# A chunked linear-attention layer with a two-layer SiLU network behind it: r and k turned in two row groups, y turned by DMA, the first chunk written out by hand

## The chip, the cores and the metric

The kernel runs on one core of one Trainium2 chip. The metric is device time in microseconds, from the start to the end of one execution. Three runs of the kernel before gave 225.85, 229.26 and 228.23 us, median 228.23. The profile is of one further execution, with a span of 226.5 us.

The engines are called by their names in the profile: PE is TensorE (matmuls), PEld its weight loads, DVE is VectorE, ACT is ScalarE, POOL is GpSimd, SP is SyncE, which here only issues DMAs. Matmul results land in PSUM[...].

## The reference

Batch 4, 8 heads, 768 tokens, head dimension 48. For each batch and head a state of 48x48 is carried from token to token:

```python
for t in range(S):
    cur = einsum('bhd,bhe->bhde', u[None] * kt, vt)
    y[:, :, t] = einsum('bhd,bhde->bhe', rt, state + cur)
    state = w[None, :, :, None] * state + einsum('bhd,bhe->bhde', kt, vt)
```

Then y is laid out as x, one row of 384 per token (3072 tokens), and goes through a network of two layers without biases:

```python
h = x @ w_in                       # 384 -> 2048
g = h * (1.0 / (1.0 + np.exp(-h))) # SiLU
out = g @ w_out                    # 2048 -> 384
```

## The kernel before, in words

**Chunks and units.** The 768 tokens are cut into six chunks of 128 (C). A unit is one chunk of one batch, all 8 heads; there are 24 (NU), and unit i is chunk i // 4, batch i % 4. Within a chunk the recurrence becomes matmuls: r is scaled by w to the power of the token's place (lamR), k by the inverse (lamK), both after being turned so that the head dimension lies on the partitions. Two heads share one turned block, at partitions 0 to 47 and 64 to 111, so there are four pairs (NP).

**One unit.** `p1_natural` works on untransposed data: v is cast to f16 on ACT, and POOL forms k times u (`ku`, L145), times r (`rku_f`, L147), k decayed to the end of the chunk (`kc`, L148) and, after DVE has summed over the head dimension (`rku`, L151), the bonus term `vu` (L153). `p1` turns r and k on PE, eight transposes of 128x112 against a 128x128 identity (L165), into two PSUM banks; DVE multiplies each with lamR and lamK while it evicts them (L167, L169); from the second chunk on ACT makes an f16 copy of r (L172). `p2` multiplies k and r of each head in f32 (L179 for the head at partition 0, L181 for the one at 64), into two banks, and DVE masks each bank to the strict triangle (`am`, L186). `p3` sums, in PSUM, r times the state (L198, from the second chunk on) and masked product times v (L201), forms the chunk's addition to the state (`sps`, L208), adds `vu` to y on DVE (L211) and updates the state (L215, L221, L224, L225). `p4` turns y on PE, three transposes (L237), and ACT copies the result to xT (L238), where the four batches of one chunk lie side by side.

**The network.** `l1` is one block of 128 hidden units for the four batches of a chunk: three matmuls of 512 columns (L248) and a SiLU on ACT (L251); 16 blocks per chunk. `l2` is four of the 16 matmuls that give one batch's output (L260, 384 columns); the last part copies the sum on DVE (L264) and stores it. So a chunk gives 16 + 16 = 32 pieces of work.

**The order.** Nothing is scheduled: each engine runs its instructions in the order of the program. The loop over units calls the product of unit i, the preparation of unit i + 1, then `p3` and `p4` of unit i, and puts between them, with `fill(n)`, pieces from the list `fillers`. That list gets the 32 pieces of a chunk when the chunk's fourth unit is done, so the pieces of one chunk fill the gaps of the next one, eight per unit; there is none before unit 4, and the pieces of the last chunk run alone at the end:

```python
for i in range(NU):
    p2(i)
    fill(2)
    ...
    load(i + NIN)
    fill(1); p3(i)
    fill(2); p4(i)
    fill(3)
    if b == B - 1:
        fill(len(fillers))
        fillers.extend(moe(sc))
```

**Loads and buffers.** r, k and v of a unit come by SP's queue (192 KB each, L102) into one of four buffers (NIN), unit 0 first, then `w_bc` and `u_bc`, then units 1 to 3; unit i + 4 is asked for once unit i's data is used. The weights come by POOL's queue, which casts them to f16: w_in in three pieces behind the first unit's work (L285), w_out in four during unit 1 (L292). PSUM: three banks for r, k and products (tag tA), two for y, state and turned y, three for the network.

Of the kernel before, what the change touches and what calls it, by code (L numbers as in the profile page):

```python
# [8 lines left out]
FP = mybir.dt.float32  # L9
# [6 lines left out]
def kernel(  # L16
# [11 lines left out]
    nc = tc.nc  # L28
# [12 lines left out]
    NIN = 4  # L41

# [5 lines left out]


    wpT = cst.tile([PR, NP], FP)  # L50
    nc.vector.memset(wpT, 1.0)
    nc.sync.dma_start(out=wpT[0:D, :], in_=bass.AP(tensor=w.tensor, offset=0,
                                                   ap=[[1, D], [PW, NP]]))
    nc.sync.dma_start(out=wpT[64:PR, :], in_=bass.AP(tensor=w.tensor, offset=D,
                                                     ap=[[1, D], [PW, NP]]))
    w_bc = cst.tile([128, HD], FP)
    u_bc = cst.tile([128, H, D], FP)

# [8 lines left out]

    maskM = cst.tile([128, 128], FP)
# [3 lines left out]
        base=-1, channel_multiplier=-1, pattern=[[1, 128]],  # L72
    )
    ident16 = cst.tile([128, 128], F16)
    nc.gpsimd.tensor_copy(out=ident16, in_=ident)


    rin = [big.tile([128, H, 64], FP, name=f"rin{i}") for i in range(NIN)]
    kin = [big.tile([128, H, 64], FP, name=f"kin{i}") for i in range(NIN)]
    vin = [big.tile([128, H, D], FP, name=f"vin{i}") for i in range(NIN)]  # L80
    kc = [big.tile([128, H, 64], F16, name=f"kc{i}") for i in range(2)]
# [5 lines left out]
    st = [big.tile([PR, NP, PW], FP, name=f"st{b}") for b in range(B)]  # L87
    st16 = [big.tile([PR, NP, PW], F16, name=f"stb{b}") for b in range(B)]
    for b in range(B):
        nc.vector.memset(st[b], 0.0)  # L90
    win = [big.tile([128, DFF], F16, name=f"win{q}") for q in range(NQ)]
    wout = big.tile([128, NFT, HD], F16)

    def unit(i):
        return divmod(i, B)

    def load(i):
        if i >= NU:
            return
        sc, b = unit(i)  # L100
        for t, src, wd in ((rin, r, 64), (kin, k, 64), (vin, v, D)):
            nc.sync.dma_start(out=t[i % NIN][:, :, 0:D],  # L102
                              in_=src[b, :, sc * C:sc * C + C, :]
                              .rearrange("h t d -> t h d"))

    load(0)
    nc.sync.dma_start(out=w_bc, in_=bass.AP(tensor=w.tensor, offset=0,
                                            ap=[[0, 128], [1, HD]]))
    nc.sync.dma_start(out=u_bc, in_=bass.AP(tensor=u.tensor, offset=0,
                                            ap=[[0, 128], [D, H], [1, D]]))  # L110
    for i in range(1, NIN):
        load(i)

# [3 lines left out]
    lnw_bc = cst.tile([128, HD], FP)  # L117
    nc.scalar.activation(out=lnw_bc, in_=w_bc, func=AF.Ln)
    eR = cst.tile([PR, NP, C], FP)
    nc.vector.tensor_tensor(out=eR, in0=it_row.unsqueeze(1).broadcast_to([PR, NP, C]),  # L120
                            in1=lnwT.unsqueeze(2).broadcast_to([PR, NP, C]), op=ALU.mult)
# [6 lines left out]
    nc.scalar.activation(out=lamK, in_=eK, func=AF.Exp, scale=-1.0)  # L128
    lamC = cst.tile([128, H, D], FP)
# [5 lines left out]

    live = {}

    def p1_natural(i):

        n = i % NIN  # L140
        L = live.setdefault(i, {})
        L["v16"] = wrk.tile([128, H, D], F16, name="v16", bufs=3)
        nc.scalar.copy(out=L["v16"], in_=vin[n])
        ku = wrk.tile([128, H, D], FP, name="ku")
        nc.gpsimd.tensor_tensor(out=ku, in0=kin[n][:, :, 0:D], in1=u_bc, op=ALU.mult)  # L145
        rku_f = wrk.tile([128, H, D], FP, name="rku_f")
        nc.gpsimd.tensor_tensor(out=rku_f, in0=rin[n][:, :, 0:D], in1=ku, op=ALU.mult)  # L147
        nc.gpsimd.tensor_tensor(out=kc[i % 2][:, :, 0:D], in0=kin[n][:, :, 0:D],  # L148
                                in1=lamC, op=ALU.mult)
        rku = wrk.tile([128, H], FP, name="rku")  # L150
        nc.vector.tensor_reduce(out=rku, in_=rku_f, axis=mybir.AxisListType.X, op=ALU.add)  # L151
        L["vu"] = wrk.tile([128, H, D], FP, name="vu")
        nc.gpsimd.tensor_tensor(out=L["vu"], in0=vin[n],  # L153
                                in1=rku.unsqueeze(2).broadcast_to([128, H, D]),
                                op=ALU.mult)

    def p1(i):
        n = i % NIN
        L = live.setdefault(i, {})
        tr = ps.tile([128, NP, C], FP, tag="tA", bufs=3)  # L160
        tk = ps.tile([128, NP, C], FP, tag="tA", bufs=3)
        for t, src in ((tr, rin), (tk, kin)):
            flat = src[n].rearrange("p h d -> p (h d)")
            for p in range(NP):
                nc.tensor.transpose(t[0:PR, p, :], flat[:, 128 * p:128 * p + PR], ident)  # L165
        L["rT"] = wrk.tile([PR, NP, C], FP, name="rT")
        nc.vector.tensor_tensor(out=L["rT"], in0=tr[0:PR], in1=lamR, op=ALU.mult)  # L167
        L["kT"] = wrk.tile([PR, NP, C], FP, name="kT")
        nc.vector.tensor_tensor(out=L["kT"], in0=tk[0:PR], in1=lamK, op=ALU.mult)  # L169
        if i >= B:  # L170
            L["rT16"] = wrk.tile([PR, NP, C], F16, name="rT16")
            nc.scalar.copy(out=L["rT16"], in_=L["rT"])  # L172

    def p2(i):
        L = live[i]
        ae = ps.tile([128, NP, C], FP, tag="tA", bufs=3)
        ao = ps.tile([128, NP, C], FP, tag="tA", bufs=3)
        for p in range(NP):
            nc.tensor.matmul(ae[:, p, :], L["kT"][0:D, p, :], L["rT"][0:D, p, :],  # L179
                             start=True, stop=True)  # L180
            nc.tensor.matmul(ao[:, p, :], L["kT"][64:PR, p, :], L["rT"][64:PR, p, :],  # L181
                             start=True, stop=True)
        L["am"] = []
        for a in (ae, ao):
            am = wrk.tile([128, NP, C], F16, name="am", bufs=4)
            nc.vector.tensor_tensor(out=am, in0=a,  # L186
                                    in1=maskM.unsqueeze(1).broadcast_to([128, NP, C]),
                                    op=ALU.mult)
            L["am"].append(am)

    def p3(i):
        sc, b = unit(i)
        L = live[i]
        v16 = L["v16"]
        y = ps.tile([128, H, D], FP, tag="y", bufs=2)
        for p in range(NP):
            if sc:
                nc.tensor.matmul(y[:, 2 * p:2 * p + 2, :], L["rT16"][:, p, :],  # L198
                                 st16[b][:, p, :], start=True, stop=False)
            for j in range(2):  # L200
                nc.tensor.matmul(y[:, 2 * p + j, :], L["am"][j][:, p, :],  # L201
                                 v16[:, 2 * p + j, :], start=not sc, stop=(not sc or j == 1))
        if sc < NCH - 1:
            sps = ps.tile([128, NP, PW], FP, tag="y", bufs=2)
            kf = kc[i % 2].rearrange("p h d -> p (h d)")
            vf = v16.rearrange("p h d -> p (h d)")
            for p in range(NP):
                nc.tensor.matmul(sps[0:PR, p, :], kf[:, 128 * p:128 * p + PR],  # L208
                                 vf[:, PW * p:PW * p + PW], start=True, stop=True)
        L["y16"] = wrk.tile([128, H, D], F16, name="y16")  # L210
        nc.vector.tensor_tensor(out=L["y16"], in0=y, in1=L["vu"], op=ALU.add)  # L211
        if sc < NCH - 1:
            if sc:
                sdec = wrk.tile([PR, NP, PW], FP, name="sdec")
                nc.gpsimd.tensor_tensor(out=sdec, in0=st[b],  # L215
                                        in1=wCT.unsqueeze(2).broadcast_to([PR, NP, PW]),
                                        op=ALU.mult)
            for p0, c0 in ((0, 0), (64, D)):
                dst = st[b][p0:p0 + D, :, c0:c0 + D]
                if sc:  # L220
                    nc.vector.tensor_tensor(out=dst, in0=sps[p0:p0 + D, :, c0:c0 + D],  # L221
                                            in1=sdec[p0:p0 + D, :, c0:c0 + D], op=ALU.add)
                else:
                    nc.vector.tensor_copy(out=dst, in_=sps[p0:p0 + D, :, c0:c0 + D])  # L224
            nc.gpsimd.tensor_copy(out=st16[b], in_=st[b])  # L225
# [3 lines left out]
    def p4(i):  # L229
        sc, b = unit(i)  # L230
        L = live.pop(i)
        if sc not in xts:
            xts[sc] = wrk.tile([128, NQ, B, C], F16, name="xT", bufs=2)
        yT = ps.tile([128, NQ, C], F16, tag="y", bufs=2)
        yf = L["y16"].rearrange("p h d -> p (h d)")
        for q in range(NQ):
            nc.tensor.transpose(yT[:, q, :], yf[:, 128 * q:128 * q + 128], ident16)  # L237
        nc.scalar.copy(out=xts[sc][:, :, b, :], in_=yT)  # L238

# [3 lines left out]
    def l1(sc, ft):  # L243
        if ft == 0:
            gts[sc] = wrk.tile([128, NFT, B * C], F16, name="gT", bufs=2)
        hps = ps.tile([128, B * C], FP, tag="moe", bufs=3)
        for q in range(NQ):
            nc.tensor.matmul(hps, win[q][:, ft * 128:(ft + 1) * 128],  # L248
# [91 lines left out]
```

## Time and profile before

| | |
|---|---|
| median of 3 runs | 228.23 us |
| span of the profile | 226.5 us |
| PE busy | 202.3 us (89%) |
| PEld busy | 133.1 us (59%) |
| POOL busy | 119.0 us (53%) |
| DVE busy | 115.8 us (51%) |
| ACT busy | 94.2 us (42%) |
| first matmul of the network | 42.8 us |
| last matmul | 222.8 us |
| DMA, mean over the span | 100 GB/s |

The profile is read in three ways here. The slices cut the span into 40 equal parts and give the busy share of each engine in tenths, PE's granted clock in tenths of full speed, and the share of the DMA engines. The stretches give busy microseconds with the number of instructions in brackets. The chain follows the work that ended last back from the end; each piece has its start, its length and what it was. Matmuls overlap in the pipeline, so the distance between the starts of two of them, not the duration of one, is what a matmul costs.

### The profile page before, as it was taken

The page shows a single profiled execution, that of the slowest core. Times are in us where ns is not written, and L with a number is a line of the kernel's source. Part 1 is how long each engine was busy: PE and PEld are TensorE (multiplying, and loading weights), DVE is VectorE, ACT ScalarE, POOL GpSimd, SP SyncE. Part 2 cuts the span into 40 slices and gives each one's busy share as a digit, 9 for nine tenths or more (in the row PEclk, how much of TensorE's full clock was granted, in tenths as well). Part 3 has the DMA queues.
Part 4 walks back from the last instruction along what each step waited for, and adds up shares of the span by engine and source line. Part 5 has one row for each costly group of instructions (what it writes and reads, how often), then busy time and mean ns, then how long its engine had stood idle before and what let it go on. Part 6 is the DMA issues. An engine that isn't in the chain of part 4 may idle for free.

```text
span 226.5 us, 4378 instructions
## 1 busy us (share of the span) xinstructions
PE 202.3 (89%) x1672; PEld 133.1 (59%) x1672; DVE 115.8 (51%) x225; ACT 94.2 (42%) x173; POOL 119.0 (53%) x150
## 2 busy tenths in 40 slices
PE   1266298799999999999999999999999999999993
PEld 1164177456667656766665776666676557654561
DVE  6157365647368536656833865563685256420020
ACT  2521011586621378411578211866213783029500
POOL 2387975765674665667467466656746561000000
PEclk9999555799999999999999999999999999999999
DMA  5999999992216385026735053923161000110011
GB/s 95 201 196 208 204 185 176 224 186 50 58 38 139 105 177 104 3 76 137 166 77 107 0 142 98 213 48 61 38 142 69 3 0 3 69 53 16 3 69 69
DMA packets 81604, 22.69 MB, mean 100 GB/s; under 512 B 75824, under 2 KB 81200, under 8 KB 81584
## 3 DMA queue, kind: packets, MB, share of 16 engines
q1 hardware_dynamic: 79040, 19.28, 39.3%
q0 software_dynamic: 2544, 3.15, 8.0%
q8 instruction: 13, 0.21, 0.4%
q14 instruction: 7, 0.06, 0.1%
HBM read 20.84 MB, written 4.72 MB: 113 GB/s over the span
## 4 chain that ended last, share of the span: by engine, by line
PE 81%; POOL 8%; DVE 3%; issue 3%; DMA 2%; SPq 1%; DVEq 0%; POOLq 0%
PE hps L248 28%; PE ops L260 28%; PE ae L179 10%; PE tr L165 4%; PE tk L165 4%; PE yT L237 2%; DMA u_bc<-in_u_dram 2%; POOL ku L145 2%; PE y L201 2%; POOL rku_f L147 2%; PE sps L208 2%; PE y L198 2%; POOL wout L292 1%; SPq L102 1%; POOL kc L148 1%
## 5 line engine op out<-in xcount | busy, mean ns | idle before, releaser
L248 PE MATMUL hps<-xT,win 128*128 128x512 f16 x288 | 70.2, 384 | 0.0
L251 ACT ACTIVATE gT<-hps 128x512 f16<-128x512 f32 x96 | 57.4, 598 | 29.5 <-PE hps L248 27.3
L260 PE MATMUL ops<-wout,gT 128*128 128x384 f16 x384 | 69.0, 326 | 0.0
L260 PEld LDWEIGHTS <-gT 128*128 128x128 f16 x384 | 35.8, 98 | 21.2
L248 PEld LDWEIGHTS <-win 128*128 128x128 f16 x288 | 26.7, 99 | 26.5 <-issue 1.3
L186 DVE TENSOR_TENSOR am<-ae,maskM 128x512 f16<-128x512 f32 x24 | 16.6, 691 | 49.1 <-PE ao L181 49.1
L153 POOL TENSOR_TENSOR vu<-vin,rku 128x384 f32<-128x384 f32 x24 | 19.9, 829 | 35.8 <-DVE rku L151 35.8
L179 PE MATMUL ae<-rT,kT 48*128 48x128 f32 x192 | 30.8, 306 | 6.1 <-DVE kT L169 6.1
L179 PEld LDWEIGHTS ae<-rT,kT 48*128 48x128 f32 x192 | 25.8, 206 | 14.2 <-issue 7.5
L264 DVE COPY osb<-ops 128x384 f32<-128x384 f32 x24 | 13.4, 557 | 38.3 <-PE ops L260 37.9
L181 PE MATMUL ao<-rT,kT 48*128 48x128 f32 x192 | 30.8, 306 | 0.0
L238 ACT COPY xT<-yT 128x384 f16<-128x384 f16 x24 | 11.4, 476 | 43.3 <-PE yT L237 43.3
L145 POOL TENSOR_TENSOR ku<-kin,u_bc 128x384 f32<-128x384 f32 x24 | 24.1, 1005 | 7.9 <-DMA u_bc<-in_u_dram 6.7
L172 ACT CAST rT<-rT 112x512 f16<-112x512 f32 x20 | 12.4, 618 | 37.2 <-DVE rT L167 37.2
L181 PEld LDWEIGHTS ao<-rT,kT 48*128 48x128 f32 x192 | 25.8, 206 | 0.0
L147 POOL TENSOR_TENSOR rku_f<-rin,ku 128x384 f32<-128x384 f32 x24 | 24.0, 999 | 1.9
L148 POOL TENSOR_TENSOR kc<-kin,lamC 128x384 f16<-128x384 f32 x24 | 24.0, 999 | 0.8 <-ACT lamC L130 0.8
L225 POOL CAST stb<-st 112x384 f16<-112x384 f32 x20 | 10.1, 503 | 25.0 <-DVE st L221 19.9
L165 PE MATMUL tr<-ident,rin 128*112 128x128 f32 x96 | 16.7, 302 | 5.1 <-DMA rin<-in_r_dram 5.1
L167 DVE TENSOR_TENSOR rT<-tr,lamR 112x512 f32<-112x512 f32 x24 | 16.5, 689 | 4.2 <-PE tr L165 4.2
L151 DVE TENSOR_REDUCE rku<-rku_f 128x8 f32<-128x384 f32 x24 | 13.1, 544 | 10.2 <-POOL rku_f L147 10.1
L165 PEld LDWEIGHTS tr<-ident,rin 128*112 128x112 f32 x96 | 12.5, 147 | 9.0 <-issue 5.9
(46 smaller groups left out, 200.9 us busy)
## 6 DMA issues: line engine op xcount, KB each, us to landing
rin<-in_r_dram SPq DMA_DIRECT2D x24, 192.0 KB, 3.4
kin<-in_k_dram SPq DMA_DIRECT2D x24, 192.0 KB, 3.5
vin<-in_v_dram SPq DMA_DIRECT2D x24, 192.0 KB, 3.6
out_dram<-osb SPq DMA_DIRECT2D x24, 192.0 KB, 1.9
win<-in_moe_w_in_dram POOLq DMA_DIRECT2D x3, 512.0 KB, 8.8
wout<-in_moe_w_out_dram POOLq DMA_DIRECT2D x4, 384.0 KB, 10.3
w_bc<-in_w_dram SPq DMA_DIRECT2D x1, 192.0 KB, 4.3
u_bc<-in_u_dram SPq DMA_DIRECT2D x1, 192.0 KB, 4.1
```

Source lines behind the costliest of these rows:

```text
L145: nc.gpsimd.tensor_tensor(out=ku, in0=kin[n][:, :, 0:D], in1=u_bc, op=ALU.mult)
L147: nc.gpsimd.tensor_tensor(out=rku_f, in0=rin[n][:, :, 0:D], in1=ku, op=ALU.mult)
L148: nc.gpsimd.tensor_tensor(out=kc[i % 2][:, :, 0:D], in0=kin[n][:, :, 0:D], in1=lamC, op=ALU.mult)
L153: nc.gpsimd.tensor_tensor(out=L["vu"], in0=vin[n], in1=rku.unsqueeze(2).broadcast_to([128, H, D]), op=ALU.mult)
L165: nc.tensor.transpose(t[0:PR, p, :], flat[:, 128 * p:128 * p + PR], ident)
L167: nc.vector.tensor_tensor(out=L["rT"], in0=tr[0:PR], in1=lamR, op=ALU.mult)
L179: nc.tensor.matmul(ae[:, p, :], L["kT"][0:D, p, :], L["rT"][0:D, p, :], start=True, stop=True)
L181: nc.tensor.matmul(ao[:, p, :], L["kT"][64:PR, p, :], L["rT"][64:PR, p, :], start=True, stop=True)
L186: nc.vector.tensor_tensor(out=am, in0=a, in1=maskM.unsqueeze(1).broadcast_to([128, NP, C]), op=ALU.mult)
L248: nc.tensor.matmul(hps, win[q][:, ft * 128:(ft + 1) * 128], xts[sc][:, q, :, :].rearrange("p b t -> p (b t)"), start=(q == 0), stop=(q == ...
L251: nc.scalar.activation(out=gts[sc][:, ft, :], in_=hps, func=AF.Silu)
L260: nc.tensor.matmul(ops, gts[sc][:, ft, b * C:(b + 1) * C], wout[:, ft, :], start=(ft == 0), stop=(ft == NFT - 1))
```

## The change

The kernel's order is rewritten, with these parts:

- **r and k turned in two row groups** (`turn`). Each transpose takes 64 tokens instead of 128; the two halves of a pair lie at partitions 0 to 63 and 64 to 127, so they use different rows of PE, and each half writes a bank of its own. The aim is that the halves run side by side. `decay` evicts from this layout.
- **y by DMA from unit 6** (`turn_y`): a transposing DMA on SP's queue writes xT straight from y, in place of three transposes on PE and a copy on ACT. Units 0 to 5 stay on PE.
- **One mask over two banks** (`masked`): the two products lie in one PSUM tile of two banks and are masked by one instruction of 1,024 elements.
- **PSUM** is cut into one pool of two double banks for turned r and k, products, and y with the state's addition (tag att), and four banks for the network.
- **The first chunk by hand**: units 0 to 3 are written out in order. The first layer of chunk 0 runs in half blocks: two hidden blocks of the first two batches in one bank (256 columns each), from unit 2 on; the other half follows as eight pieces in `fillers`. The weights come in four pieces of 512 columns and four of w_out, spread between the units.
- **The start**: one table for ln and exp is loaded at once, w and u come by ACT's queue, the loads of units 0 to 3 are first on SP's; POOL instead of DVE clears the states; DVE instead of POOL decays k in units 0 to 3; the first chunk's state is copied by ACT.
- **Smaller ones**: the state's matmul takes 128 columns of kc instead of 112; the decayed state is formed ahead of its unit; the output's copy moves from DVE to ACT except for the last chunk; the loop gives two and six pieces instead of two, one, two and three, and doesn't empty the list at a chunk's end.

```diff
+    def turn(i):
         n = i % NIN
-        tr = ps.tile([128, NP, C], FP, tag="tA", bufs=3)
-        tk = ps.tile([128, NP, C], FP, tag="tA", bufs=3)
-        for t, src in ((tr, rin), (tk, kin)):
+        t = L(i)["t"] = ps.tile([128, 2, 2, NP, HC], FP, name="t", tag="att", bufs=2)
+        for x, src in enumerate((rin, kin)):
             flat = src[n].rearrange("p h d -> p (h d)")
             for p in range(NP):
-                nc.tensor.transpose(t[0:PR, p, :], flat[:, 128 * p:128 * p + PR], ident)
+                for y in range(2):
+                    rows = slice(HC * y, HC * y + HC)
+                    nc.tensor.transpose(t[0:PR, y, x, p, :], flat[rows, 128 * p:128 * p + PR],
+                                        ident[rows, rows])
...
+    def masked(i):
+        am = L(i)["am"] = wrk.tile([128, 2, NP, C], F16, name="am")
+        nc.vector.tensor_tensor(
+            out=am.rearrange("p h g c -> p (h g) c"), in0=L(i)["a"].rearrange("p h g c -> p (h g) c"),
+            in1=maskM.unsqueeze(1).broadcast_to([128, H, C]), op=ALU.mult)
...
-                nc.tensor.matmul(sps[0:PR, p, :], kf[:, 128 * p:128 * p + PR],
+                nc.tensor.matmul(sps[:, p, :], kf[:, 128 * p:128 * p + 128],
                                  vf[:, PW * p:PW * p + PW], start=True, stop=True)
...
+    def turn_y(i, by_pe):
+        sc, b = unit(i)
+        yf = L(i)["y16"].rearrange("p h d -> p (h d)")
+        x = x_tile(sc)
+        if not by_pe:
+            nc.sync.dma_start_transpose(out=x[:, :, b, :], in_=yf)
+            return
...
+    def l1(sc, b0, nb, ft):
...
+        m = B // nb
+        hps = ps.tile([128, m, nb * C], FP, name="hps", tag="moe", bufs=4)
+        for f in range(m):
+            for q in range(NQ):
+                nc.tensor.matmul(hps[:, f, :], win[:, q, (ft + f) * 128:(ft + f + 1) * 128],
+                                 xts[sc][:, q, b0:b0 + nb, :].rearrange("p b t -> p (b t)"),
+                                 start=(q == 0), stop=(q == NQ - 1))
...
+    bonus_products(0)
+    ld_win(0)
+    turn(0)
+    decay(0)
+    cast_v(0)
+    product(0)
+    turn(1)
+    bonus_sum(0)
+    bonus_v(0)
+    masked(0)
+    decayed_k(0)
+    decay(1)
+    bonus_products(1)
+    ld_win(1)
+    outputs(0)
+    evict_y(0)
+    product(1)
+    turn_y(0, True)
+    state(0)
+    load(4)
...
+    fillers.extend([lambda ft=ft: l1(0, 2, 2, ft) for ft in range(0, NFT, 2)])
+    fillers.extend(second(0))
+
+    for i in range(B, NU):
+        sc, b = unit(i)
+        product(i)
+        if i + 1 < NU:
+            bonus_products(i + 1)
+            decayed_k(i + 1)
+        masked(i)
         fill(2)
         if i + 1 < NU:
-            p1_natural(i + 1)
-            p1(i + 1)
+            turn(i + 1)
+            decay(i + 1)
+        outputs(i)
+        evict_y(i)
+        turn_y(i, i < 6)
+        state(i)
         load(i + NIN)
...
+        fill(6)
         if b == B - 1:
-            fill(len(fillers))
-            fillers.extend(moe(sc))
+            fillers.extend(first(sc) + second(sc))
     fill(len(fillers))
```

## The prediction

> **What bounds the kernel now.** I read the page's forty slices first, then the busy time of three long stretches, the waits of TensorE, and the chain of work, in order of time, through one unit of the steady part.
>
> ```profile
> PE   1266298799999999999999999999999999999993
> PEclk9999555799999999999999999999999999999999
> DMA  5999999992216385026735053923161000110011
> ```
>
> A slice is 5.66 us. TensorE is below full for the first seven or eight and full to the end after that; its clock is at half in slices five to seven; the DMA engines are full in slices two to nine.
>
> ```profile
> 0.00:20.00 20.00, 6.72 (x46) 5.64 (x47) 9.65 (x27) 5.86 (x10) 10.95 (x22) 1.00 0.86 170
> 20.00:42.90 22.90, 15.63 (x137) 12.91 (x137) 12.72 (x26) 4.78 (x9) 16.92 (x21) 0.61 1.14 196
> 42.90:222.80 179.90, 179.90 (x1493) 114.51 (x1492) 92.90 (x172) 83.53 (x155) 91.09 (x108) 0.99 0.36 81
> ```
>
> Columns: stretch, length, busy time of PE, PEld, DVE, ACT and POOL, granted clock, DMA share, GB/s. From 42.9 us TensorE never idles; no other engine is busy much over half of that stretch. Before it TensorE is busy 22 of 43 us, partly at half clock.
>
> ```profile
> PE yT L237 <- DVE y L211: 9.4, 4, 4.5
> PE ae L179 <- DVE kT L169: 6.1, 1, 6.1
> PE tr L165 <- DMA rin<-in_r_dram: 5.1, 1, 5.1
> ```
>
> These are all the waits TensorE has, and all lie in the first 43 us. So there are two accounts: what TensorE has to do, and when it can begin to do it without a break. One steady unit, from the chain:
>
> ```profile
> 59.14 0.30 PE ae L179
> 59.44 0.01 PE ao L181
> 59.45 0.11 PE ae L179
> ...
> 60.23 1.41 PE ops L260 x8
> 61.64 0.44 PE tr L165 x4
> 62.07 0.44 PE tk L165 x4
> 62.51 0.65 PE ops L260 x4
> ...
> 63.54 0.23 PE sps L208 x4
> 63.77 1.30 PE ops L260 x8
> 65.07 0.17 PE yT L237 x3
> 65.23 1.95 PE ops L260 x12
> 67.18 0.30 PE ae L179
> ```
>
> The unit takes 67.18 - 59.14 = 8.04 us: product of k and r 1.09, turning of r and k 0.88, outputs 0.38 (63.16 to 63.54), state 0.23, y turned 0.17, and eight fillers of 0.65 (5.2), of which the one after the product shows 0.11 more.
>
> **What the Trainium skill says.** "TensorE: Matmul & The Clock Gate", Part 1: the clock is halved until the array has been busy for some microseconds, and again after an idle window. The trace agrees: steps of 0.11 us in the product above are 0.21 us at 29 us, with the clock row at 5. The same page, on weight-path perf modes: a fast weight load is taken for 128 weight columns that are not fp32. The trace agrees (weight loads between 60 and 200 us):
>
> ```profile
> L165 PEld LDWEIGHTS tr<-ident,rin 128*112 128x112 f32 x68 | 8.2, 133 | 2.4
> L201 PEld LDWEIGHTS <-am 128*128 128x128 f16 x144 | 7.8, 97 | 1.6
> L208 PEld LDWEIGHTS <-kc 128*112 128x112 f16 x56 | 3.9, 130 | 0.0
> ```
>
> 112 columns take 130 ns in f16 and 133 in f32; 128 columns in f16 take 97. "TensorEngine Tiling (Array Packing)", Key Properties: tiles in different row groups run in parallel, and changing the tiling mode drains the array. Both are in the trace: the even and odd product start 0.01 us apart, and its first step is 0.30 instead of 0.11, with 0.11 more behind the block. Eight pairs at 0.107 would be 0.86; the block costs 1.20. So a block in row groups pays about 0.3 us of entry and exit.
>
> **The change part by part.**
>
> TensorE's account. Warm work before: 179.9 us after 42.9, and before that four whole units of the first chunk plus turn and product of unit 4. A unit of the first chunk is 0.88 + 1.20 + 0.26 (outputs without the state's part, my share of the 0.38) + 0.23 + 0.17 = 2.74; 4 x 2.74 + 0.88 + 1.20 = 13.0. Sum 192.9.
>
> *Turning in two row groups*: 16 transposes of 64 rows by 64 columns in place of 8 of 128, the pair side by side. A transpose of 128 columns takes 0.11 (0.44 for four), so 64 columns 0.055; if the pair is truly parallel, weight loads too, the block is 8 x 0.056 + 0.3 = 0.75. If the two weight loads take turns, each about 0.05 (112 columns in f16 keep a 0.057 pace in the state's four matmuls, 0.23 for four), the pair costs 0.10 and the block 8 x 0.10 + 0.3 = 1.1. Today 0.88 without any switch. I take no change; the bounds are 24 x -0.13 = -3 us and 24 x +0.2 = +5 us.
>
> *y by DMA from unit 6*: 18 x 0.17 = 3.1 us less. *State matmul with 128 weight columns*: the pace falls from 0.057 to 0.04 (96 columns; output matmuls of 96 columns show 0.04 to 0.05), 20 x 0.06 = 1.2 less. *Half blocks*: 256 columns cost half of 512 (0.215), so the sum stays. Work after: 192.9 - 3.1 - 1.2 = 188.6.
>
> Off the path in steady state: one mask over two banks (1,024 elements: 0.69 + 512 / 0.96 = 1.2 us by the scaling of the 512 operations, instead of 0.69 + 0.68) lies under two fillers and the turn, 1.3 + 0.9; the output's copy moved to ScalarE (0.5 us each) finds it with 83.5 of 179.9 us busy, less 0.48 per unit for the xT copy that goes; the shared pool of two double banks asks only for order that the data asks for anyway, since the turn of i+1 reuses what was evicted one filler block earlier. All are hidden by TensorE's 7.5 to 8 us per unit.
>
> The start. Loads are issued first on SyncE, at about 1 us instead of 1.9; w and u go on ScalarE's queue behind one table load (1.28). By the landing of about 2 us for w, 4.1 for u: w at 5, u at 7.5. lnw 5.3, eR 6.1, lamR 6.8 and lamK 7.5 (the second table load, 1.28 at 8.93, is gone, and neither waits for w_bc, which cost 3.5), decay to 8.3: first product at 8.3, against 13.04. The cleared states on GpSimd (eight, about 0.4 each by VectorE's 0.38 today) lie under the wait for u, 6.7 us today. After that the cycle of a first unit is VectorE's: mask 1.2, decayed k 0.55, decay 1.37, then product on TensorE (1.2, up to 2 at half clock) while y and the bonus sum (0.55 each) run: 4.5 to 5.5 us. GpSimd has 1.0 + 1.0 + 0.83 + about 0.8 of issue, less than that; today it carries also kc 1.0, the state's cast and seven issues in lumps of 1.8 and 3.1. Products of units 1 and 2 at about 13.7 and 19; first half blocks at about 21. From there TensorE has per unit 1.2 + 0.88 + 0.5 + 0.17 + 2.6 of half blocks = 5.3, as much as VectorE's cycle, so it is full. With 1.7 us for the clock that rises late: effectively full from 22.7, having done 2 x 2.74 + 0.88 + 1.20 = 7.6.
>
> Bubbles added: the table load before the first Silu, 1 us (1.28, half hidden by four buffers). DMA: until the second layer starts in unit 5, loads 0 to 5 (3.54 MB), w and u (0.4) and both weights (3.15) = 7.1 MB must land; at the 190 to 196 GB/s seen, 37 us, from 2 us on 39; unit 5 is due at about 38. I take 2 us. Unit 7: fillers of chunk 0 are 8 + 16 = 24, used up by units 4 to 6, so unit 7 has none, and chunk 1 can't begin before its y came by DMA. Mask 1.2, outputs 0.4, decay and y 2, transfer 3 to 4, less product 1.2 and turn and next product 2: about 4 us idle. At the other four ends of a chunk six fillers (3.9) and a product (1.2) stand between outputs and the first use of xT: 5.1, against decay's rest and y 1.6 plus the transfer.
>
> *The transfer itself* is in no row. From below: a plain store of 192 KB lands in 1.9 us, so 1.9. From above: "VectorE: DVE Perf Modes", The three transpose paths, prices a 128x128 crossbar transpose at 1309 ns; three one after the other give, as an estimate, 3.9. I take 3.9: 0.4 to 0.7 us of wait, 4 x 0.7 = 2.8. Queued behind it on SyncE are only loads for four units later, which have a unit to spare.
>
> Sum: 22.7 + 188.6 - 7.6 = 203.7; + 1 + 2 + 4 + 2.8 = 213.5 for TensorE's end. The tail (copy and store, 226.5 - 222.8) stays 3.7, giving 217. Counted from the DMA side: second layer at 41, with 26.2 us of work done by then (sixteen half blocks 10.4, five units 13.7, turn and product 2.1): 41 + 188.6 - 26.2 + 4 + 2.8 + 3.7 = 214. The two share their terms; I take 215.
>
> **Rivals.** *The start stays bound by DMA* (0.15): the full DMA row up to slice nine speaks for it; if both weights land as late as today's DMA row ends, 50 us, the end is 50 + 188.6 - 26.2 + 4 + 2.8 + 3.7 = 223. Against it: today nothing of the weights was issued before 13.7, and GpSimd's lumps delayed it. *All parts work* (0.14): parallel transposes (-3), transfer in 1.9 (-2.8, and -2 in unit 7), no DMA bubble (-2): 205. *The transposing transfer becomes the bound* (0.06): two-byte pieces at, say, 9 us each put 5 us on each of five chunk ends and hold the loads behind them; with the turn at its upper bound (+5) and the late DMA that is 223 + 5 x 3 + 5 = 243, slower. Nothing in the profile speaks for it but that no such transfer is in it.
>
> **How the numbers follow.** The forecast has 0.65. Range 205 to 223: it holds the forecast with its bounds (turn -3 to +5), the first two rivals at their ends, and leaves the last out. Two per cent are 223.7 and 232.8: faster 0.88, same 0.07, slower 0.05.
>
> **What would show it.** Right: product of unit 0 at 8 to 9 us, first Silu at 21 to 24, TensorE's slices full from the fifth, one idle gap near unit 7, a unit of 7.5 to 7.9 us. Turn: block time against 0.88. Transfer: time to landing, and waits of the first layer on it once per chunk. Wrong: weights landing after 45 us, first-layer matmuls waiting for xT by more than 2 us at every chunk, or a turn above 1.1 us.

## The result, and the profile after

The changed kernel took 214.36 us (median of 4 runs, 213.84 to 214.56), the kernel before, measured beside it, 228.29. The ratio is 0.942, with a 95% interval of 0.936 to 0.948: faster by about 6%. 215 was predicted. The profiled execution has a span of 212.6 us. Medians here and below are of all runs, while ratios and their intervals leave out executions in a slower state, of which only the kernel before and one experiment on it have some.

The slices of the changed kernel, each 5.3 us long:

```profile
PE   1677898798986999999999999999999999999993
PEclk9999999999998899999999999999999999999999
DMA  6899999999175255277346267525627010220011
```

TensorE is at seven to nine tenths from the third slice, with a dent in the thirteenth (63.8 to 69.1 us), and full after it. The stretches tell how much of each part it was busy (columns as before the change: length, PE, PEld, DVE, ACT, POOL, clock, DMA share, GB/s):

```profile
0.00:22.65 22.65, 12.65 (x127) 10.24 (x127) 14.62 (x29) 6.86 (x16) 17.11 (x33) 1.00 0.94 170
22.65:43.70 21.05, 19.13 (x227) 15.47 (x226) 11.97 (x19) 16.41 (x37) 15.56 (x19) 1.00 1.18 196
43.70:60.60 16.90, 15.65 (x166) 10.23 (x165) 8.29 (x14) 4.38 (x9) 9.25 (x12) 1.00 0.57 122
60.60:69.10 8.50, 5.50 (x72) 3.76 (x74) 5.28 (x8) 2.11 (x4) 6.75 (x9) 0.92 0.77 173
69.10:188.30 119.20, 119.20 (x1163) 72.19 (x1164) 60.62 (x100) 59.22 (x108) 69.40 (x82) 0.99 0.45 100
```

The first matmul of the network starts at 22.65 us instead of 42.8. From there to 69.1 TensorE idles 1.92 + 1.25 + 3.0 = 6.2 us, where before it idled not at all after 42.9; from 69.1 to the last matmul it never idles. Its two longest waits in that part (total, times, longest), and from the chain the work behind the second, at the end of unit 7:

```profile
PE yT L283 <- DVE y L248: 3.2, 3, 1.3
PE hps L295 <- DMA xT<-y: 1.6, 1, 1.6
```

```profile
67.00 2.09 PE hps L295 x6
69.09 1.03 PE t L187 x16
```

A steady unit, from the chain of the changed kernel (start, length, work; the outputs in between are left out):

```profile
98.02 1.09 PE a L207 x16
99.11 1.40 PE hps L295 x6
100.51 0.59 PE t L187 x16
101.10 0.15 PE ys L223
...
101.59 0.17 PE ys L235 x4
101.76 3.88 PE hps L295 x18
105.64 1.09 PE a L207 x16
```

The unit takes 105.64 - 98.02 = 7.62 us, where it was 8.04. The turn of r and k is 0.59 (0.88 before), but in the chain the first output matmul behind it shows 0.15, where the kernel before has this:

```profile
63.16 0.04 PE y L198
```

That is 0.11 more for a block in row groups, and it leaves a net gain of 0.18. The state's four matmuls take 0.17 (0.23), and y's 0.17 is gone. Together these are 0.41, the difference of the units but for rounding. The transfer that took y's place, from the list of DMA issues (count, median us to landing):

```profile
xT<-y SPq DMA_TRANSPOSE x18, 2.3
```

### The profile page after: what moved, and what is told of

Read it like the earlier page. It is cut to its first block, busy times and chain, and to the rows that moved or that the text cites. A ratio compares the mean times of both kernels' runs of the same rounds, so it can differ in the third digit from the quotient of the medians.

```text
span 212.6 us, 4734 instructions
## 1 busy us (share of the span) xinstructions
PE 192.9 (91%) x1858; PEld 122.7 (58%) x1858; DVE 103.0 (48%) x173; ACT 99.0 (47%) x190; POOL 118.1 (56%) x151
## 4 chain that ended last, share of the span: by engine, by line
PE 86%; DVE 5%; DMA 3%; issue 2%; POOL 1%; ACT 0%; ACTq 0%; DVEq 0%; POOLq 0%
PE hps L295 31%; PE ops L307 30%; PE a L207 12%; PE t L187 7%; DMA u_bc<-in_u_dram 2%; PE ys L223 2%; PE ys L228 2%; DVE rT L193 2%; PE ys L235 1%; DMA xT<-y 1%; DVE y L248 1%; PE yT L283 1%; DVE am L212 1%; DVE kT L193 1%; DVE kc L161 1%
## 5 line engine op out<-in xcount | busy, mean ns | idle before, releaser
L295 PE MATMUL hps<-xT,win 128*128 128x512 f16 (+1 forms) x336 | 68.2, 357 | 2.1 <-DMA xT<-y 1.6
L212 DVE TENSOR_TENSOR am<-a,maskM 128x1024 f16<-128x1024 f32 x24 | 29.4, 1224 | 56.1 <-PE a L207 56.0
L207 PE MATMUL a<-rT,kT 48*128 48x128 f32 x384 | 30.6, 304 | 3.4 <-DVE kT L193 3.4
L207 PEld LDWEIGHTS a<-rT,kT 48*128 48x128 f32 x384 | 25.8, 204 | 10.8 <-issue 6.5
L193 DVE TENSOR_TENSOR rT<-t,lamR 112x512 f32<-112x512 f32 x24 | 16.5, 689 | 20.6 <-PE t L187 14.7
L157 POOL TENSOR_TENSOR rku_f<-rin,ku 128x384 f32<-128x384 f32 x24 | 24.6, 1025 | 1.9
L312 ACT COPY osb<-ops 128x384 f32<-128x384 f32 x20 | 9.6, 480 | 29.3 <-PE ops L307 29.3
L193 DVE TENSOR_TENSOR kT<-t,lamK 112x512 f32<-112x512 f32 x24 | 16.3, 680 | 0.0
L187 PE MATMUL t<-ident,rin 64*112 64x64 f32 x192 | 11.6, 247 | 5.1 <-DMA rin<-in_r_dram 4.2
L248 DVE TENSOR_TENSOR y<-ys,vu 128x384 f16<-128x384 f32 x24 | 13.2, 548 | 1.8 <-PE ys L235 1.1
L242 POOL TENSOR_TENSOR sdec<-st,wCT 112x384 f32<-112x384 f32 x16 | 13.2, 828 | 0.0
```

Of the source, the lines that this page charges most:

```text
L157: nc.gpsimd.tensor_tensor(out=L(i)["rku_f"], in0=rin[n][:, :, 0:D], in1=ku, op=ALU.mult)
L187: nc.tensor.transpose(t[0:PR, y, x, p, :], flat[rows, 128 * p:128 * p + PR], ident[rows, rows])
L193: nc.vector.tensor_tensor(out=L(i)[key].rearrange("p g (y t) -> p y g t", y=2), in0=L(i)["t"][0:PR, :, x], in1=lam.rearrange("p g (y t) -> ...
L207: nc.tensor.matmul(a[:, j, p, :], kT[r0:r0 + D, p, :], rT[r0:r0 + D, p, :], start=True, stop=True)
L212: nc.vector.tensor_tensor(out=am.rearrange("p h g c -> p (h g) c"), in0=L(i)["a"].rearrange("p h g c -> p (h g) c"), in1=maskM.unsqueeze(1 ...
L248: nc.vector.tensor_tensor(out=L(i)["y16"], in0=y, in1=L(i)["vu"], op=ALU.add)
```

## The experiments

What was put to the test is the theory that TensorE is the bound nearly everywhere, so that each part is worth what it takes off or adds to TensorE's sum, idle time included, against the rivals named with each run. All times are medians with the range of 4 runs, to be set against 214.36 for the changed kernel, or against the kernel before where that was edited. The kernel before took 228.29 beside the changed kernel, and 228.36, 228.53 and 228.98 beside the three groups of experiments; differences below about 0.7 us between groups say nothing.

**Whole transposes again.**

```diff
...
-                for y in range(2):
-                    rows = slice(HC * y, HC * y + HC)
-                    nc.tensor.transpose(t[0:PR, y, x, p, :], flat[rows, 128 * p:128 * p + PR],
-                                        ident[rows, rows])
+                nc.tensor.transpose(t[0:PR, x, p, :], flat[:, 128 * p:128 * p + PR], ident)
...
```

> The changed kernel with one thing undone: r and k turned by 8 transposes of 128 tokens, r into one bank and k into the other, as before the change. Theory A (TensorE is the bound, and the row groups save 0.29 us per turn but cost 0.11 us of exit in the outputs behind it): a steady unit of 7.64 + 0.18 = 7.82 us, the time up by 24 x 0.18 = 4 us, to about 218.7. Theory B (the change of tiling mode eats what the halves win, as the prediction took it): no change, 214.4 within 1 us. Theory C (the whole 0.29 counts): up by 7 us, 221.

Measured 220.34 (219.43 to 220.6), and a steady unit of 7.82 us. Its turn in the chain, and the output behind it:

```profile
97.02 0.87 PE t L185 x8
97.89 0.04 PE ys L218
```

The unit is theory A's; theory B, which was the prediction's own choice, falls. The time rose by 6, not by 4, and so lies nearer to theory C's 221; but C asks for a unit of 7.9, and the output behind the turn is back at 0.04 from 0.15, so the 0.11 does count. The profiles show where the rest comes from. Their spans differ by 6.3 us, and the first layer starts 2.05 us later (24.70 against 22.65). About 1.2 of that is `u`, which landed 6.17 us after its issue in this execution and 4.97 in the other; it was issued at 1.94 us in both, and nothing that the edit touches stands ahead of it. The rest is a turn that takes 1.97 instead of 1.12 while TensorE is at half pace. Until unit 7 another 1.5 us come, half of it from one more slow turn (1.71 instead of 1.03). The steady units behind it give 15 x 0.18 = 2.7. So some 5 us are the edit's: 4.3 was the right sum for full pace, and at half pace a turn saves more. How `u` landed in the runs without a profile is not known.

**The halves one after the other.**

```diff
-        for x, src in enumerate((rin, kin)):
-            flat = src[n].rearrange("p h d -> p (h d)")
-            for p in range(NP):
-                for y in range(2):
-                    rows = slice(HC * y, HC * y + HC)
+        for y in range(2):
+            rows = slice(HC * y, HC * y + HC)
+            for x, src in enumerate((rin, kin)):
+                flat = src[n].rearrange("p h d -> p (h d)")
+                for p in range(NP):
```

> The changed kernel with the same 16 transposes of 64 tokens per turn, but first the eight of tokens 0 to 63, then the eight of tokens 64 to 127, so that neighbours use the same rows of TensorE. Theory A (the gain is that the two row groups run side by side, pairs of 0.07 us): one at a time they take about 0.055 each, 16 x 0.055 = 0.9 us against 0.59, the unit 7.64 + 0.3 = 7.9 us, the time up by about 7 us to 221. Theory B (the smaller transposes alone are what is cheap): the block stays at 0.6 us and the time at 214.4 within 1 us.

Measured 221.45 (220.72 to 222.81), the unit 7.92 us; the chain:

```profile
97.93 0.86 PE t L187 x16
98.79 0.15 PE ys L223
```

Theory A holds: these are the same instructions in another order, and they cost 7 us more. One at a time a half costs 0.86 / 16 = 0.054; side by side a pair costs 0.59 / 8 = 0.074, so running together saves a third, not a half. The 0.11 behind the turn is paid in both. Halves without pairs are worse than whole transposes (0.86 + 0.11 against 0.87): the new turn lives on the alternation alone.

**Pieces spread over unit 7.**

```diff
-        fill(6)
+        fill(6 if i >= 2 * B else 4)
```

> The changed kernel with four pieces instead of six after each of units 4 to 7, so that the 24 pieces of the first chunk last through unit 7 (six per unit). Theory A (unit 7 costs 3 us of idle TensorE because it has no pieces, and 1.5 us of halved clock behind it): the gap goes, the time falls by 4 to 5 us to about 210. Theory B (the gap only moves: with fewer pieces each of units 4 to 7 waits for its own chain on VectorE, or the data is late anyway): 213 to 215.

Measured 211.16 (210.4 to 211.59). The first layer waits for no transfer any more, and the dent is gone from TensorE's slices. This is theory A, with 3.2 us instead of 4 to 5; in the profiled execution `u` landed 1.0 us later than in that of the changed kernel.

**No half blocks.**

```diff
-    for ft in range(0, 4, 2):
-        l1(0, 0, 2, ft)
...
-    fillers.extend([lambda ft=ft: l1(0, 2, 2, ft) for ft in range(0, NFT, 2)])
-    fillers.extend(second(0))
+    fillers.extend(first(0) + second(0))
```

> The changed kernel without the half blocks in units 2 and 3: the first layer of chunk 0 runs as 16 whole blocks of 512 columns from unit 4 on, so that the first chunk has 32 pieces again, eight for each of units 4 to 7. Theory A (units 0 to 3 are paced by VectorE and the loads; the half blocks there fill time but units 2 to 4 get longer and unit 7 has no pieces, so what is won early is given back in unit 7): 211 to 215, no loss against 214.4. Theory B (the half blocks are what the start gains): 5 us of TensorE's work move behind the start, 218 to 220.

Measured 215.59 (215.32 to 215.74), 1.2 above the changed kernel and 0.6 outside theory A's band, but far from B's. The first layer starts at 34.8 us instead of 22.65, and unit 7 has no gap. Set against the run before this one, which has no gap either, the half blocks are worth 215.59 - 211.16 = 4.4 us. In the changed kernel unit 7 took 3.2 of them back.

**y on TensorE throughout.**

```diff
-        turn_y(i, i < 6)
+        turn_y(i, True)
```

> The changed kernel with y turned by TensorE in all 24 units (three transposes and a copy on ScalarE), no transposing DMA. Theory A (the DMA takes 0.17 us per unit off TensorE and is hidden except in unit 7): units 6 to 23 longer by 0.17, together +3.1 us, less about 1.5 us in unit 7, where turning on TensorE is faster than the 2.3 us of the transfer: 215.5 to 217. Theory B (the transfer costs as much as it saves, by waits or by the loads queued behind it): 213 to 215, or less.

Measured 240.77 (240.14 to 241.08). Both theories fail, by 24 us. The longest of TensorE's waits, and then part of one unit in the chain:

```profile
PE yT L283 <- DVE y L248: 25.6, 21, 1.4
```

```profile
98.63 0.61 PE t L187 x16
...
100.53 0.56 DVE y L248
101.09 0.05 issue
101.14 0.34 PE yT L283 x3
```

After the outputs TensorE's next instruction is the turn of y, and VectorE gets to y only behind the decay of r and k. In the changed kernel the instruction that waits for y is a DMA on SyncE's queue, and TensorE goes on. The kernel before had two pieces between outputs and turn.

**The same with two pieces ahead of the turn.**

```diff
         evict_y(i)
-        turn_y(i, i < 6)
+        fill(2)
+        turn_y(i, True)
...
-        fill(6)
+        fill(4)
```

> The changed kernel with y turned by TensorE in all units, as in the run that took 240.8 us, but with two of the six pieces moved ahead of the turn of y in units 4 to 23, so that VectorE has time to add the bonus to y. Theory A (the 26 us were TensorE waiting for VectorE, 1.3 us a unit, since nothing stood between outputs and the turn; the transposes themselves cost 0.17): 215 to 217. Theory B (turning y on TensorE is dear in this order whatever stands ahead of it): over 230.

Measured 216.17 (215.79 to 217.55): theory A. The other 24.6 us were the wait. The 1.8 that remain are a net figure. A unit is 7.94 us, 0.32 longer and not 0.17, because y is still finished 0.1 us after the two pieces are; in return units 4 and 5 no longer wait for y, and in unit 7 the first layer waits for no transfer.

**The kernel before with the new turn alone.** VectorE evicts each bank by itself there.

```diff
...
+        t = [ps.tile([128, 2, NP, HC], FP, name=f"t{y}", tag="tA", bufs=3) for y in range(2)]
...
+                for y in range(2):
+                    rows = slice(HC * y, HC * y + HC)
+                    nc.tensor.transpose(t[y][0:PR, x, p, :], flat[rows, 128 * p:128 * p + PR],
+                                        ident[rows, rows])
...
```

> The kernel before with one part of the change: r and k turned in two row groups of 64 tokens, each half into a bank of its own; VectorE evicts with four operations of 256 elements instead of two of 512. Theory A (0.18 us per unit off TensorE's sum, and in the first units, at half clock, hidden behind other waits): the 20 units after the first chunk give 20 x 0.18 = 3.6 us, 224 to 225.5 against 228.3. Theory B (the halves gain only beside the changed order of the other kernel): no change, 228.

Measured 225.97 (224.75 to 226.46) against 228.53, ratio 0.990 (0.983 to 0.997). That is 0.5 us outside theory A's band and not B. The unit is 7.86 us, 0.18 less, as in the changed kernel:

```profile
70.48 0.59 PE t L167 x16
71.07 0.76 PE ops L269 x4
```

The piece of four matmuls behind the turn took 0.65 before. What is missing lies at the start. From the first layer to the last matmul the profile is 3.1 us shorter, but the first layer starts at 43.9 instead of 42.9. TensorE has a wait there that the kernel before doesn't have, for the mask; that this wait alone makes the 1 us was not tested:

```profile
PE t L167 <- DVE am L195: 2.7, 4, 0.7
```

**The kernel before with y by DMA alone, from unit 6.**

```diff
+        yf = L["y16"].rearrange("p h d -> p (h d)")
+        if i >= 6:
+            nc.sync.dma_start_transpose(out=xts[sc][:, :, b, :], in_=yf)
+            return
...
```

> The kernel before with one part of the change: y by DMA from unit 6. Its order has two pieces between outputs and the turn of y, so TensorE never waited there. Theory A (the DMA saves the transposes alone): 18 x 0.17 = 3.1 us less, 225 to 226 against 228.4. Theory B (the DMA's worth in the changed kernel, over 20 us, comes with the DMA and not with the order): 215 or less. Theory C (the transfer is late at the ends of chunks, where three pieces and a product, 3.1 us, stand ahead of the first layer): 228 or more.

Measured 227.11 (225.84 to 229.31, 20 runs) against 228.98 (23 runs), ratio 0.996 (0.993 to 0.9995). The ratio allows a gain of 0.1 to 1.6 us, of the 3.1 that theory A named. The trace has a new wait of the first layer for xT, at two ends of chunks:

```profile
PE hps L251 <- DMA xT<-y: 1.3, 2, 0.7
```

At both the transfer was issued behind a store that itself waited for VectorE's copy of the output. B falls. 3.1 - 1.3 = 1.8 is still a little more than the interval allows, so A holds only in part, and what C named, a late transfer, did come, though it takes back a part of the gain and not all of it.

**y by DMA from unit 4, with the pieces spread.**

```diff
-        turn_y(i, i < 6)
+        turn_y(i, i < 4)
...
-        fill(6)
+        fill(6 if i >= 2 * B else 4)
```

> The changed kernel with four instead of six pieces after units 4 to 7 (211.2 us by itself), and y by DMA from unit 4 instead of 6. Theory A (TensorE stands still for 1.2 us in unit 4 until VectorE has y, and turns y in 0.34 and 0.17 us in units 4 and 5; the next chunk's first layer needs neither before unit 8): 1.5 us less than with the even filling alone, 209.5. Theory B (the DMA engines are full until about 50 us and the transfer or the loads behind it come late): 211 or more.

Measured 207.32 (206.54 to 208.52), ratio to the kernel before 0.909 (0.901 to 0.918): 3.8 less than spreading alone, more than theory A's 1.5. The waits of TensorE for y fell from 3.2 us to 0.7. That is 2.5, since units 4 and 5 both waited (1.20 and 1.25), while theory A counted unit 4 alone. The two turns of y, 0.34 each in the chain, are gone too. Between the profiled executions 1.0 more is the landing of `u` (5.96 and 4.94 us after its issue). Theory B fails as to the time. But the transfer of unit 4, which went out while the DMA engines were full, held SyncE's queue for 4.2 us instead of 1.2, and the slowest transfer of the run took 5.7 to landing; unit 4's data has until unit 8.

**Decayed k of the first units on GpSimd.**

```diff
-        eng = nc.vector if i < B else nc.gpsimd
+        eng = nc.gpsimd
```

> The changed kernel with the decayed k of units 0 to 3 on GpSimd, as before the change, instead of on VectorE. Theory A (on VectorE it takes 0.65 to 1.42 us instead of the predicted 0.55 because it waits for GpSimd's operations[...], and it stands in the chain between the mask and the next decay): VectorE's cycle falls by 1.0 to 1.4 us in units 0 and 1, the first half block comes 1.5 to 2.5 us earlier and the time falls by as much, to 212 to 213. Theory B (GpSimd is the pace of the first units): its 1.0 us per unit delays the bonus products, no change or slower, 214 to 217.

Measured 214.15 (213.16 to 215.05): no difference in time that can be told, which is theory B's number. In the profile the first half block comes at 21.69 instead of 22.65. On VectorE the four operations had taken (min/median/max, ns, from the instructions of their line in the changed kernel):

```profile
L161 DVE TENSOR_TENSOR kc<-kin,lamC x4: 650/1166/1422, 10.8 to 30.6; 128x384 f16<-128x384 f32 x4
```

So theory A's reason is there and its size is not. Only the first cycle became shorter, from 6.0 to 4.7 us between products; in the next the operation had run beside the turn, which waits for the mask to free the shared pair of banks anyway, and the cycle is 6.0 with it and without it.

**The three edits together.**

> The changed kernel with the three edits that did not lose: four pieces after units 4 to 7, y by DMA from unit 4, decayed k on GpSimd throughout. Theory A (the gains are in different stretches and add): 207.3 less the 0.2 to 1.1 us that the last edit gave alone, 206 to 207. Theory B (GpSimd's extra work in the first units is felt once TensorE is full earlier): 207.3 or more.

Measured 208.14 (207.67 to 210.59), no better than 207.32; the ranges overlap. The profiled execution is the slowest of the four, and in it the first layer waits for xT:

```profile
PE hps L295 <- DMA xT<-y: 2.9, 2, 2.3
```

The transfer of unit 7 is queued on SyncE behind stores and a load that waits for GpSimd. The number is theory B's. That GpSimd's extra work in the first units is the reason is not shown, and the wait explains this one execution, not the median.

**And TensorE kept busy at the start.** The three edits, and 26 matmuls whose result nobody reads:

```diff
+    def warm(n):
+        x = ps.tile([128, 128], FP, name="warm", tag="moe", bufs=4)
+        for _ in range(n):
+            nc.tensor.matmul(x, ident16, ident16, start=True, stop=True)
...
     ld_win(0)
+    warm(12)
     turn(0)
+    warm(14)
...
```

> The same as the run with the three edits together, and 26 matmuls of 128x128 in f16 that compute nothing used: 12 before and 14 behind the turn of unit 0, while TensorE waits for data. Theory A (in the first 25 us the products take 2.1 us instead of 1.1, the turns 1.1 instead of 0.6 and the first half blocks 2.7 instead of 1.3, all in the chain, because the clock is halved; keeping TensorE busy from 2.5 us on lifts that): products of units 0 to 2 at 1.1 us and 3 to 4 us less than the run with the three edits. Theory B (the waits between the first units are long enough that the clock falls back, or other waits take the place): less than 1 us.

Measured 206.17 (205.62 to 207.54), ratio 0.906 (0.899 to 0.913). That is 2.0 less than the three edits, between the two theories, and the lowest median of all, though its range overlaps that of 207.32. Theory A's mechanism failed all the same. The products of units 0, 2 and 3 in TensorE's order of time (start, duration; other work in between left out):

```profile
7.67 2.08 PE L207 MATMUL a<-rT,kT 48*128 48x128 f32 x16 [0.62 <-DVE kT L193]
...
18.91 2.08 PE L207 MATMUL a<-rT,kT 48*128 48x128 f32 x16 [0.60 <-DVE kT L193]
...
27.10 1.16 PE L207 MATMUL a<-rT,kT 48*128 48x128 f32 x16
```

TensorE is at half pace until 24.6 us, as without the extra matmuls. The first half block is at 21.99 against 22.11. What the 2 us are is open: the wait for xT doesn't occur in this execution, but why was not tried.

## Why the prediction was right, step by step

The total was right within 1 us, while its terms were off by as much as 4.3 us, in both directions.

*TensorE's sum.* 192.9 - 3.1 - 1.2 were predicted, and nothing for the turn. y and the state came as worked out. **The turn failed**: 24 x 0.18 = 4.3 us less instead of 0. The step that failed is "I take no change" between a block of 0.75 and one of 1.1: measured 0.59 + 0.11 = 0.70, below even the lower bound. A pair costs 0.074, so the two weight loads do not take turns at 0.05 each; and the 0.3 us of entry and exit, taken over from the product block, is 0.11 here. The chain books it behind the turn. By the starts of the matmuls it lies ahead of it: six matmuls of the layer take 1.30 (18 take 3.88), and the first transpose starts 1.40 behind the first of them. So the size is shown and the place is not:

```profile
99.04 1.47 PE L295 MATMUL hps<-xT,win 128*128 128x512 f16 x6
100.44 0.43 PE L187 MATMUL t<-ident,rin 64*112 64x64 f32 x8
```

So the sum is 184.3.

*When TensorE is full.* Products of units 0 to 2 were predicted at 8.3, 13.7 and 19 us; the chain of the changed kernel:

```profile
1.94 4.97 DMA u_bc<-in_u_dram
...
10.83 1.42 DVE kc L161
...
13.59 2.10 PE a L207 x16
15.71 1.24 DVE am L212
16.99 1.12 PE t L187 x16
...
19.57 2.08 PE a L207 x16
...
22.65 2.72 PE hps L295 x12
```

The first product was at 7.56, earlier; the cycle is 6.0 us, not 4.5 to 5.5. In the first cycle the reason is decayed k, predicted at 0.55. The Trainium skill, "SBUF — State Buffer", Terms, says that VectorE and GpSimd share a pair of ports which one of them holds for a whole instruction. This trace agrees: each of the first three operations ended 0.4 us after the GpSimd operation that it met, whenever it had begun, so they took 1.42, 1.03 and 0.65 us. The first two, each below the GpSimd operation:

```profile
10.82 1.00 POOL L155 TENSOR_TENSOR ku<-kin,u_bc 128x384 f32<-128x384 f32 x1
10.83 1.42 DVE L161 TENSOR_TENSOR kc<-kin,lamC 128x384 f16<-128x384 f32 x1
16.47 1.00 POOL L155 TENSOR_TENSOR ku<-kin,u_bc 128x384 f32<-128x384 f32 x1 [1.19 <-DMA kin<-in_k_dram]
16.85 1.03 DVE L161 TENSOR_TENSOR kc<-kin,lamC 128x384 f16<-128x384 f32 x1
```

In the second cycle it is the turn, which stands between mask and decay and was not in the predicted chain. In every cycle it is also the product at half pace, 2.1 us in each of the three, the upper end of what was allowed. The first Silu, behind a table load of 1.28 us, began at 25.4 and not at 21 to 24, the sign that was named.

*The bubbles.* Done by 22.65 were 2 x (2.74 - 0.18) + 0.70 + 1.20 = 7.0 us; 22.65 + 184.3 - 7.0 = 199.9, and TensorE ended at 209.1. So 9.2 us were lost behind the start; 1 + 2 + 4 + 2.8 + 1.7 (clock) = 11.5 were predicted, in other places. The weights by DMA cost nothing, nor did the table load before the first Silu: TensorE waits for none of them. Instead it waits 3.2 us for y in units 3 to 5, which was not in the prediction: the order leaves nothing between outputs and the turn of y. Unit 7 was right in kind and near in size: 3.0 us idle, and some 1.6 of half pace behind it (the first six matmuls of the layer take 2.09 instead of 1.30, the turn 1.03 instead of 0.59, outputs and state 1.07 instead of 0.66), 4.6 against 4. The rest is half pace at the start: the first twelve matmuls take 2.72 instead of 1.3. At the other ends of chunks 0.7 us each were predicted and nothing was lost, since the transfer lands after 2.3 us. The price from the Trainium skill, "VectorE: DVE Perf Modes", The three transpose paths, 1309 ns per 128x128 and three in a row, 3.9, was too high here: the measurement, 2.3 for all three blocks, decides.

*The change's 14 us*, then: 4.3 + 3.1 + 1.2 = 8.6 from TensorE's sum, and the rest from the start. Before, at 42.9 us, 13.0 us of work were done, so 29.9 were lost; now 22.65 - 7.0 = 15.6, a gain of 14.3, of which the 9.2 us of later bubbles were given back. 8.6 + 14.3 - 9.2 = 13.7, and the last matmul came 222.8 - 209.1 = 13.7 earlier. The two agree by construction, as the 9.2 is what was left over; that most of it has a wait or a slow stretch in the trace is what speaks for the account.

*Where luck helped.* TensorE's end was predicted at 213.5 and came at 209.1: 4.3 less from the turn, 2.2 more from the start (15.6 lost instead of 21 - 7.6 = 13.4), 2.3 less from the later bubbles. And the prediction's sums, 217 and 214, are spans, as is its tail of 226.5 - 222.8; the device time is 1.7 us longer than the span in both kernels. So the two accounts stood for 218.9 and 215.7, and the 215 that was taken between them came nearer than either.

*y by DMA* was priced at its 0.17 us per unit. That is right as a part of TensorE's sum, and it misses what the DMA does in this order: it is what allows the turn of y to follow the outputs at once. With the turn on TensorE in that place the kernel would have been slower than before (240.8); in an order that leaves room for it the DMA is worth 1.8. No part of the prediction asked what the removed instruction would have waited for in the new order.

*The rivals.* The start bound by the DMA of the weights did not come: the DMA row is still full to the tenth slice, but no matmul waits for a weight. Yet another transfer sets the start, the 192 KB of `u`, with which the chain begins. In the five profiled executions whose first units are the same program (this kernel, and the runs with the pieces spread, with y by DMA from unit 4 and the two with y on TensorE) `u` landed at 6.91, 7.90, 6.89, 7.31 and 8.06 us and the first half block began at 22.65, 23.63, 22.62, 23.04 and 23.79, each time 15.7 later. In the run with decayed k alone moved to GpSimd the chain begins with `w` instead. An earlier `u` was not tried. *All parts work* nearly came in its parts (the turn won even more than 3, the transfer and the weights cost nothing at the ends of chunks and in the second layer), but not in its 205: the later start and the waits for y, which it didn't have, took that back. The transfer as the bound did not come.

## What to carry to other kernels

Where one engine is full, keep two accounts, its sum of work and the time at which it can start without a break, and look behind the start for what is given back: here a stretch without pieces took back 3.2 of the 4.4 us that starting early had won. A part can be worth far more than its instructions' time when it moves a wait from a full engine to a queue that has time; test it by undoing it in place, and then with room made for it. Halving an operation to use two row groups paid here only with the halves alternating. Before an early start is explained by engines, look at the first transfer of the chain in several executions.

## What the runs showed of the hardware

Transposes of 64 rows by 112 columns in f32 in two row groups took 0.074 us a pair, against 0.054 for one alone and 0.11 for a whole one of 128 rows. A block of them cost 0.11 us more than its transposes. A transposing DMA of 128x384 in f16 took 1.19 us of SyncE's queue and landed 2.3 us after its issue (medians); among full DMA engines one took 4.2 us of the queue. A VectorE operation with two inputs in SBUF, 128x384, ended 0.4 us after the GpSimd operation that it met, so it took 0.65 to 1.42 us. 26 small matmuls between 2.5 and 7 us, followed by f32 products and transposes with gaps of up to 1 us, did not lift TensorE from half pace; full pace came after 2.6 us of f16 matmuls without a gap from 22 us on. The clock row of the page reads 9 in all that time: the pace of the matmuls has to be taken from their spacing.
